# Two heads in one pair of tiles, and values loaded 2 MB at a time, in a decode step with its gradients

## The chip, the cores and the metric

One core of one Trainium2 chip. The metric is the device time of one execution in microseconds (us); lower is better. The number shown for a kernel is the median of its runs.

## What is computed

A decode step (one token, batch of 2) of a block whose attention and bilinear feed-forward part stand side by side, and the gradients of its output with respect to its input, the caches and all weights:

```python
# B, Sq, D = 2, 1, 576; Hq, Hkv, Sk, Dh = 32, 16, 4096, 128; F = 4608; all bfloat16
xn = _layernorm(x, axis=-1)
q = (xn @ wq) per head;  k, v = caches, each shared by 2 query heads
p = softmax(q k^T * Dh**-0.5);  A = (p v) @ wo
B = ((xn @ w_gate) * (xn @ w_up)) @ w_down
out = x + A + B
# outputs: out, and the vjp with grad_out for
#   x, k_cache, v_cache, wq, wo, w_gate, w_up, w_down
```

Each cache is 2 x 16 x 4096 x 128 bfloat16, 32 MB, and is read once. Its gradient has the same size and is written once: each row of it is a sum of outer products, of probabilities (for v) or score gradients (for k) with a vector of the query head.

## The kernel before

**Order.** The function is a set of Python generators (streams). Each yields requests (an operation with an estimated time, a buffer to acquire, an event to wait for), and `Order.run` goes through them while the kernel is built and emits the instructions of each engine in the order in which its model of the engines would start them. So the order on every engine, and on SP's queue, which issues nearly all transfers, is fixed at build time. The model's constants (`LATENCY`, `RATE`, `LAG` and so on), the priorities `PRI`, the places `AT` where weights are loaded and the caps on buffers set that order. `Line.push` models when a transfer lands. `ACQ(tag)` takes one free slot of a ring, `REL` gives it back, `SET` and `WAIT` mark events; the waits on the chip itself follow from the data.

**Buffers.** 16 tiles of 1 MB, [128, 4096] bfloat16 (`big`, `NBIG`), are shared by four users with caps: loads of keys and values (`kv`, 7), their transposed copies (`X`, 15), gradients waiting to be stored (`st`, 4) and the weights of the feed-forward part (`G`, 2).

**Steps.** `NS` = 16 steps: 8 groups of two key heads times 2 batches. In a step, each head's keys and values are loaded (`load_kv`, 1 MB each): partition p holds 32 consecutive positions, a row of 8 KB. `turn` makes a transposed copy with two DVE transposes per tile (line 418). `score` multiplies it with a stationary made by `build_W` (line 1205, into PSUM). `softmax` normalizes; `spread` (lines 1212 and 1213) and a DVE transpose bring the probabilities into `pp`, two blocks of [128, 128]: one as the stationary of the outer products, one of the contraction with the values. `dscore` does the same for the score gradients into `dd`. `contract` (line 1378) multiplies them with the loaded tiles. `outer` and `head_outer` make the gradient of the caches: matmuls (line 1226) with a block diagonal `BD` of 16 blocks, 8 for each head, built by GpSimd (line 1193) with `mask16`; PSUM is copied to `big` tiles by ACT or DVE (`cp`, lines 422 and 424, whichever the model finds earlier) and stored by `put` (line 644) 1 MB at a time. `consts` builds the masks and selectors on DVE before the first step. Beside the steps run the feed-forward part (`mlp`), the projections of a group (`group_front`, `group_back`) and the gradients of the weights (`rows_outer` and others), which share all engines.

Of the kernel before, what the change touches and what calls it, by code (L numbers as in the profile page):

```python
# [9 lines left out]
ALU = mybir.AluOpType  # L10
# [42 lines left out]
class Line:  # L53
    def __init__(self):
        self.end = 0.0

    def push(self, at, work):
        if at > self.end:
            self.end = at + (DRY if at > self.end + 0.3 else 0.0)
        self.end += work  # L60
        return Landing(self.end + LAG + DRIFT * self.end)


class Order:
# [58 lines left out]
    def start(self, s):  # L123
# [15 lines left out]
        if r[0] == "acq":  # L139
            ts = [when(t) for t in self.pool(r[1]).values() if t is not None]  # L140
            if not ts or (r[1] in self.used and self.used[r[1]] >= self.cap[r[1]]):
                return None, None
            return max(s.ready, min(ts)), None
# [9 lines left out]
    def run(self):  # L153
        while self.streams:
# [27 lines left out]
            elif r[0] in ("wait", "gate"):  # L182
                s.ready = t
            elif r[0] == "acq":
                slots = self.pool(r[1])
                if r[1] in self.used:
                    self.used[r[1]] += 1
                i = min((k for k, v in slots.items() if v is not None), key=lambda k: (when(slots[k]), k))
                slots[i] = None
                s.ready = t  # L190
                value = i
            elif r[0] == "dma":
                self.free[e] = t + r[2]
                s.land = self.line.push(t + r[2] + LATENCY, r[3])
# [30 lines left out]
def ACQ(tag):  # L225
    return ("acq", tag)
# [22 lines left out]
def DMA(engine, cost, nbytes, row=8192):  # L249
    return ("dma", engine, cost, 0.01 + RATE * nbytes / 16e3 * (0.03676 + 8.0 / row))  # L250
# [3 lines left out]
NBIG, NGU, NWW, NBD = 16, 1, 6, 3  # L254
CAP = {"kv": 7, "X": 15, "st": 4, "G": 2}
PRI = {
    "turn0": [12127.5, 6592.3, 21769.7, -2605.1, 16027.7, 11327.0, 15999.3, 39550.4, 10382.6, -7734.4, 35538.2,
        24878.1, 2718.9, 31584.2, -26890.5, 2784.8],
    "turn1": [-17638.3, 2610.3, 11642.0, -23025.1, -666.2, 15183.7, -8429.9, 1153.7, -20487.3, 25941.4,
        10117.7, 4947.3, -2272.2, 26485.5, 30929.5, -2450.0],  # L260
    "W0": [17499.7, 23187.9, 23229.4, -24562.1, -25413.4, 21241.8, -52583.1, 25355.3, -4026.7, -26992.9,
        -2792.0, -39509.0, -20712.1, -23397.7, -38581.5, -1973.1],
    "W1": [-68220.0, -3785.6, -5692.6, -26672.7, -32830.2, -16110.0, -12761.0, -19860.2, 22087.6, 15126.8,
        -21980.3, 8805.5, -32643.6, 50340.4, -9766.7, -46949.6],
    "BD0": [33847.1, 15885.5, -3782.4, -11229.3, 24201.3, 31507.4, 16705.2, 36715.7, 22613.4, -26234.1,
        -2581.7, 109848.8, -44765.9, -8040.0, -3442.2, 23039.7],
    "BD1": [6023.1, 63457.9, 25871.9, 3200.3, 32198.5, -18814.1, 12365.4, 26532.9, 45847.1, -51895.6, 27362.3,
        -76393.3, 2863.2, -15443.1, -42340.1, -14044.7],
    "att": [-30329.0, -12134.6, -9680.1, 2262.2, -4349.2, 5413.2, -20317.8, -14023.7, -15815.4, -22206.1,
        -49797.4, -334.9, -19593.2, -20211.8, -68161.8, -27358.0],  # L270
    "dsc": [-23906.4, -34630.7, -2728.5, -23998.0, -19328.5, -8575.3, -10061.5, -15550.8, 13655.4, -23902.2,
        -28324.1, -40880.7, -28538.6, -56867.0, -5830.5, -12006.5],
    "conv": [-12341.8, -11809.0, -28772.8, 4652.6, -75297.7, -7012.1, -20664.5, 17461.5, 27449.8, 21658.4,
        -6850.8, -13921.3, -10206.6, -13431.8, 19855.6, -8570.5],
    "con": [-42900.2, 17788.3, 198.2, -17106.1, -21976.4, -3999.9, 7207.3, -22623.4, -6927.6, 21516.2, 20924.0,
        -13390.2, -118243.2, -7700.5, 19019.7, 14780.5],
    "out0": [22678.2, 12788.2, 42398.2, 31027.3, 49279.4, -11087.6, 5917.5, 42793.0, -20399.7, 57105.8,
        29375.6, 687.4, 24906.2, -2550.4, -27276.1, 33869.5],
    "out1": [19262.8, 2604.4, 2928.7, 23228.2, 21627.8, -10501.4, 15188.8, 7961.4, 18967.4, 20607.5, 11898.0,
        33332.1, 33685.2, 22220.0, 30731.2, 4846.1],  # L280
    "load": [27975.6, -31596.9, -27237.7, 3512.0, -22563.4, -17007.1, 4137.9, 25122.5, 5758.3, -9052.6,
        -35105.2, 2003.7, -28928.7, 6812.9, 23298.4, -60102.7],
    "front": [22268.9, 9016.8, -3195.4, -925.0, -11488.9, -5594.5, -10266.7, 2816.4],
    "back": [8334.8, 3131.5, 10704.4, -20159.0, -16008.9, -4698.0, -5371.8, 1371.3],
    "mlp": [-5535.1, -15193.4, -221.7, -14784.7, -3773.2, 8812.5, 807.2, 180.8, 6936.3],
    "mload": [-52363.2, -31069.0, 25120.7, -76464.9, 11215.5],
    "wload": [26545.8, -25483.3, -28807.4, 17849.2, -51701.7, -14210.9, -857.7, -9350.9, -12979.9, -24368.0,
        -173571.7, -10429.5, -11015.2, 13337.1, -10805.0, 6634.5],
    "wout": [-3917.3],
    "store": [6257.1],  # L290
    "fin": [-45349.8],
    "const": [46567.9],
}
AT = {
    "wq": [-5, 7, 11, 24, 31, -18, 50, -5],
    "wo": [-13, -2, -15, 2, 36, -14, 47, 53],
    "mlp": [2, 16, -13, 39, 111],
}
LATENCY, DRY, RATE = 0.5, 0.9, 1.009
LM, LAG, DRIFT = 0.67, 2.2, 0.009  # L300
CLK = 1.65
BIAS = 0.21111771427708687
SLACK = {"PE": 0.0, "ACT": 0.11786185086953341, "DVE": 0.44815392421950667, "POOL": 1e9, "SP": 1e9}
# [7 lines left out]
def kernel(  # L311
# [35 lines left out]
    WW = 40  # L347
# [20 lines left out]
    kv_t = X_t = st_t = G_t = tiles("big", NBIG, [P, NCH * Dh])  # L368
# [5 lines left out]
    BD_t = tiles("BD", NBD, [P, 16, Dh])  # L374
    vr_t = tiles("vr", 2, [P, Dh])
    W_t = [tiles(f"W{t}", 2, [P, 4, G, WW]) for t in range(2)]
# [14 lines left out]
    pp_t = tiles("pp", 2, [P, 2, P])  # L391
    dd_t = tiles("dd", 2, [P, 2, P])
# [3 lines left out]
    for i in range(2):  # L396
# [4 lines left out]
            ds=const.tile([P, P], BF16, name=f"ds{i}"), sp=const.tile([P, 2 * P], BF16, name=f"sp{i}")))  # L401
        ch_t[i]["mr"] = ch_t[i]["sp"][0:1].bitcast(FP32)
# [66 lines left out]
    identP = const.tile([P, P], BF16, name="identP")  # L469
# [4 lines left out]
    S64 = ch_t[0]["ex"][:, 0:64]  # L474
    G4 = const.tile([P, 32, 4], FP32, name="G4")
    mask8 = const.tile([P, 4, 2], FP32, name="mask8")
    mk16 = ch_t[0]["ex"][:, 64:80].rearrange("p (l c) -> p l c", l=2)
    mask16 = const.tile([P, 16], BF16, name="mask16")
# [8 lines left out]
    def consts():  # L487
# [3 lines left out]
        def sums(t, dims, off=0, src=identf):  # L491
            nc.vector.reduce_sum(t, view(src[:], 0, P, off, dims), axis=AX.X)

        yield DVE(0.6)
        sums(K4[:], [[1, 4], [4, 32]])
        nc.vector.tensor_copy(G4[:], view(K4[:], 0, P, 0, [[0, 32], [1, 4]]))
        yield DVE(0.7)
# [1036 lines left out]
```

## Time and profile before

| | |
|---|---|
| median of 3 runs | 471.11 us (470.17 to 472.08) |
| profiled execution: time / span | 471.37 / 469.6 us |
| mean granted TensorE clock | 0.71 |
| bytes read and written | 92.48 MB each |

The span runs from the first to the last instruction of the profiled execution. A profile names an engine's work by line: L1226 is line 1226 of the kernel. PE is TensorE's matmul, PEld its weight load, DVE VectorE, ACT ScalarE, POOL GpSimd and SP SyncE, whose queue (SPq) issues the transfers. In a group, the number after the bar is busy time in all, then the mean of one in ns, then the idle time just before it and what ended that.

### The profile page before, as it was taken

To read this page: it belongs to the slowest core of one execution; us is meant where nothing else is said; L and a number is where in the kernel's file an instruction comes from. 1 tells how busy PE (TensorE), PEld (TensorE's weight loads), DVE (VectorE), ACT (ScalarE), POOL (GpSimd) and SP (SyncE) were. 2 spreads that over 40 slices of the span, in tenths; PEclk is the share of its full clock that TensorE was granted. 3 is DMA by queue.
4 is the path that set the end of the run, shared out by engine and by line. 5 is a ranking of instruction groups with operands and counts; after the bars stand their busy time and mean duration, and the time that the engine had idled before them with its cause. 6 is when DMAs were issued, how large, how long until landed. Compare 5 with 4: busy or idle time off the path is not lost.

```text
span 469.6 us, 15459 instructions
## 1 busy us (share of the span) xinstructions
PE 370.8 (79%) x6636; PEld 217.5 (46%) x6636; DVE 369.5 (79%) x705; ACT 334.3 (71%) x507; POOL 146.8 (31%) x176
## 2 busy tenths in 40 slices
PE   0588688869887777986997669789699898998984
PEld 0455444435653352554463444564345434444453
DVE  9689878967867879688689658978867978898772
ACT  2149668867885948671798638877678678789973
POOL 3350242681330320203252264000843705325100
PEclk9978897767757668776675767956656658566977
DMA  8999999999999999999999999999999989999995
GB/s 317 404 413 403 363 390 419 409 416 421 418 416 420 399 421 406 412 415 419 399 418 404 386 418 424 408 413 342 413 416 393 424 270 416 423 413 413 424 368 176
DMA packets 40053, 185.96 MB, mean 396 GB/s; under 512 B 3496, under 2 KB 11184, under 8 KB 23600
## 3 DMA queue, kind: packets, MB, share of 16 engines
q1 hardware_dynamic: 39976, 184.96, 98.1%
q8 instruction: 52, 0.85, 0.7%
q14 instruction: 17, 0.14, 0.1%
q10 hardware_dynamic: 8, 0.00, 0.0%
HBM read 92.48 MB, written 92.48 MB: 394 GB/s over the span
## 4 chain that ended last, share of the span: by engine, by line
PE 42%; ACT 18%; DVE 18%; DMA 12%; issue 5%; POOL 2%; SPq 2%; ACTq 0%; DVEq 0%; POOLq 0%
ACT big L422 15%; DMA out_dram<-big 10%; DVE big L418 8%; PE ps_m L1378 8%; PE ps_o L1226 7%; PE ps_m L1205 7%; PE ps_o L675 4%; PE ps_m L841 3%; DVE big L424 3%; DMA big<-in_A_v_cache_dram 3%; PE ps_m L967 2%; PE ps_m L636 2%; POOL BD L1193 2%; PE ps_o L712 1%; SPq L1129 1%
## 5 line engine op out<-in xcount | busy, mean ns | idle before, releaser
L422 ACT CAST big<-ps_o 128x1024 bf16<-128x1024 f32 (+4 forms) x319 | 279.7, 950 | 40.3 <-PE ps_o L1226 18.2
L418 DVE STREAM_TRANSPOSE big<-big 128x1024 f32<-128x1024 f32 x146 | 176.1, 1223 | 5.9 <-DMA big<-in_A_v_cache_dram 3.6
L1193 POOL TENSOR_TENSOR BD<-vr,mask 128x2048 bf16<-128x2048 bf16 x32 | 115.2, 3603 | 198.8 <-ACT vr L422 122.2
L424 DVE CAST big<-ps_o 128x1024 bf16<-128x1024 f32 (+2 forms) x71 | 78.2, 1102 | 15.8 <-PE ps_o L675 5.2
L1205 PE MATMUL ps_m<-big,W 128*32 128x128 bf16 x2048 | 57.1, 274 | 5.5 <-ACT osb L422 0.7
L1226 PE MATMUL ps_o<-BD,dd 32*128 32x512 bf16 x256 | 48.8, 489 | 12.7 <-ACT big L422 9.2
L1205 PEld LDWEIGHTS <-W 128*32 128x32 bf16 x2048 | 45.4, 121 | 21.9 <-issue 18.6
L1226 PE MATMUL ps_o<-BD,pp 32*128 32x512 bf16 x256 | 42.1, 461 | 10.4 <-ACT big L422 6.7
L1170 POOL COPY W<-rep 32x16 bf16<-32x16 bf16 x128 | 24.5, 192 | 63.5 <-DVE rep L951 53.2
L418 DVE STREAM_TRANSPOSE big<-ww 128x1152 f32<-128x1152 f32 (+1 forms) x25 | 32.9, 1317 | 4.5 <-DMA out_dram<-big 3.3
L1378 PE MATMUL ps_m<-big,pp 128*32 128x512 bf16 x256 | 28.2, 536 | 1.5 <-DVE small L1330 1.2
L1378 PE MATMUL ps_m<-big,dd 128*32 128x512 bf16 x256 | 27.5, 518 | 1.5 <-DVE dd L418 0.6
L1226 PEld LDWEIGHTS <-dd 32*128 32x128 bf16 x256 | 11.8, 97 | 32.4 <-issue 24.7
L1226 PEld LDWEIGHTS <-pp 32*128 32x128 bf16 x256 | 10.4, 95 | 26.9 <-issue 22.6
L422 ACT CAST osb<-ps_m 128x512 bf16<-128x512 f32 x15 | 8.9, 590 | 15.9 <-PE ps_m L1378 12.6
L675 PE MATMUL ps_o<-dyr,R 32*32 32x288 bf16 x256 | 17.3, 402 | 2.0 <-ACT big L422 2.0
L675 PE MATMUL ps_o<-dyr,hb 32*32 32x288 bf16 x288 | 16.5, 346 | 1.1 <-ACT big L422 0.9
L967 PE MATMUL ps_m<-big,Wdy 128*128 128x128 bf16 x144 | 14.9, 285 | 3.1 <-DVE small L1283 2.0
L712 PEld LDWEIGHTS <-xnr 32*128 32x128 bf16 x368 | 12.5, 119 | 9.3 <-issue 8.6
L422 ACT CAST sp<-ps_m 128x256 bf16<-128x256 f32 x22 | 8.4, 380 | 11.2 <-PE ps_m L1213 11.0
L636 PEld LDWEIGHTS <-wm 128*32 128x32 bf16 x704 | 13.4, 115 | 6.3 <-issue 5.1
L841 PE MATMUL ps_m<-big,Wdy 128*128 128x128 bf16 x162 | 15.6, 272 | 0.6 <-DVE small L1291 0.4
(210 smaller groups left out, 481.9 us busy)
## 6 DMA issues: line engine op xcount, KB each, us to landing
out_dram<-big SPq DMA_DIRECT2D x74, 1024.0 KB, 12.1
big<-in_A_k_cache_dram SPq DMA_DIRECT2D x32, 1024.0 KB, 12.4
big<-in_A_v_cache_dram SPq DMA_DIRECT2D x32, 1024.0 KB, 12.5
out_dram<-big SPq DMA_DIRECT2D x17, 576.0 KB, 11.4
ww<-in_B_w_down_dram SPq DMA_DIRECT2D x9, 576.0 KB, 11.1
ww<-in_A_wo_dram SPq DMA_DIRECT2D x8, 576.0 KB, 11.1
ww<-in_A_wq_dram SPq DMA_DIRECT2D x8, 512.0 KB, 11.6
big<-in_B_w_gate_dram SPq DMA_DIRECT2D x4, 1024.0 KB, 13.1
```

The lines of the kernel that those rows point to most:

```text
L418: nc.vector.transpose(out, in_)
L422: nc.scalar.copy(out, in_)
L424: nc.vector.tensor_copy(out=out, in_=in_)
L636: nc.tensor.matmul(dp[32 * q:32 * q + 32, :], lhsT=view(Wm[:], 0, P, 8 * pos(q, s), [[1, 32]]), rhs=view(X, 0, P, xoff(q, s), [[FS, blocks ...
L675: nc.tensor.matmul(o[32 * q:32 * q + 32, aa, 0:HD2], lhsT=view(t, 32 * q, 32, 2 * A + aa, [[4, 32]]), rhs=dyr[32 * q:32 * q + 32, k * HD2: ...
L841: nc.tensor.matmul(dh, lhsT=Wdy[:, e, 2 * k:2 * k + P], rhs=view(X[:], 0, P, 64 * k + e, [[D, FC], [2, 32]]), start=(k == 0 and e == 0), s ...
L967: nc.tensor.matmul(dp, lhsT=Wdy[:, e, 2 * k:2 * k + P], rhs=view(X[:], 0, P, 64 * k + e, [[D, GH], [2, 32]]), start=(k == 0 and e == 0), s ...
L1170: nc.gpsimd.tensor_copy(view(W_t[t][w][:], 32 * a, 32, 6 + 8 * a, [[G * WW, 4], [WW, G], [1, 2]]), view(rep_t[grp[g]["qs"]][:], 32 * a, 32 ...
L1193: nc.gpsimd.tensor_tensor(BD_t[i][:], view(vr_t[v][:], 0, P, 0, [[0, 16], [1, Dh]]), view(mask16[:], 0, P, 0, [[1, 16], [0, Dh]]), ALU.mult)
L1205: nc.tensor.matmul(sc[32 * cq:32 * cq + 32, :], lhsT=view(W[:], 0, P, (be * G + l) * WW + 6 - 4 * c2 - 2 * l, [[1, 32]]), rhs=view(X[:], 0 ...
L1226: nc.tensor.matmul(o[:, k, :], lhsT=pr2[32 * c4:32 * c4 + 32, :], rhs=BD[32 * c4:32 * c4 + 32, 8 * l + 4 * h2:8 * l + 4 * h2 + 4, :], star ...
L1378: nc.tensor.matmul(ct[32 * j:32 * j + 32, :], lhsT=view(rT, 0, P, 4 * c + 2 * l, [[1, 32]]), rhs=kv_t[kvS[s][t][l]][:, Dh * c:Dh * (c + 4) ...
```

## The change

A step's two heads now share a pair of neighbouring `big` tiles: each head has 64 partitions and 64 consecutive positions in each, a row of 16 KB, of which the first tile of the pair holds the first half and the second the second. With `JOINED`, the values of every step are one transfer of 2 MB in rows of 16 KB, for which two neighbouring slots are taken at once. Keys are two transfers of 1 MB and the gradients' stores two of 1 MB, in rows of 8 KB that lie 16 KB apart (`PAIRED`, for stores of 2 MB, is empty). Since a tile now has both heads, 64 partitions each, the block diagonal has 8 blocks in place of 16 for the same matmuls; the stationary of the scores has no index for the head; and the spread makes three matmuls, of 128, 128 and 256 columns, into four blocks of `pp` and `dd`, so that its copy and its transpose have 512 columns. There are 4 `BD` tiles (3 before), caps of 8 for `kv` and 6 for `st`, other constants and masks, and two clocks in `Line`, one with dearer stores. All priorities, the places of the weights and the model's constants are other numbers, so the order is another one on every engine.

```diff
 class Line:
...
-    def push(self, at, work):
-        if at > self.end:
-            self.end = at + (DRY if at > self.end + 0.3 else 0.0)
-        self.end += work
-        return Landing(self.end + LAG + DRIFT * self.end)
+    def push(self, at, work, more):
+        for k, w in enumerate((work, work + more)):
+            if at > self.end[k]:
+                self.end[k] = at + (DRY if at > self.end[k] + 0.3 else 0.0)
+            self.end[k] += w
+        return Landing(max(self.end[0] + LAGM, self.end[1] + LAG))
...
+                if r[2] == 2:
+                    i = min((k for k in range(0, len(slots) - 1, 2) if slots[k] is not None and slots[k + 1] is not None),
+                            key=lambda k: (max(when(slots[k]), when(slots[k + 1])), k))
+                    slots[i] = slots[i + 1] = None
+                    value = [i, i + 1]
...
-NBIG, NGU, NWW, NBD = 16, 1, 6, 3
-CAP = {"kv": 7, "X": 15, "st": 4, "G": 2}
+NBIG, NGU, NWW, NBD = 16, 1, 6, 4
+JOINED = [range(0), range(16)]
+PAIRED = [range(0), range(0)]
+CAP = {"kv": 8, "X": 15, "st": 6, "G": 2}
 PRI = {
...
-LM, LAG, DRIFT = 0.67, 2.2, 0.009
+LM, LAG, LAGM, SLOW = 0.67, 2.0, 3.2, 0.065
...
-    kv_t = X_t = st_t = G_t = tiles("big", NBIG, [P, NCH * Dh])
+    H2 = NCH * Dh
+    pair_t = [const.tile([P, H2 * min(2, NBIG - 2 * i)], BF16, name=f"big{i}") for i in range((NBIG + 1) // 2)]
+    kv_t = X_t = st_t = G_t = [pair_t[i // 2][:, H2 * (i % 2):H2 * (i % 2) + H2] for i in range(NBIG)]
...
-    BD_t = tiles("BD", NBD, [P, 16, Dh])
+    BD_t = tiles("BD", NBD, [P, 8, Dh])
...
-    pp_t = tiles("pp", 2, [P, 2, P])
-    dd_t = tiles("dd", 2, [P, 2, P])
+    pp_t = tiles("pp", 2, [P, 4, P])
+    dd_t = tiles("dd", 2, [P, 4, P])
...
-        nc.vector.tensor_copy(identP[:].rearrange("p (a c i) -> p a c i", a=4, i=8),
-                              view(ident[:], 0, P, 0, [[8, 4], [32, 4], [1, 8]]))
...
+        for j in range(2):
+            for a in range(4):
+                nc.vector.tensor_copy(view(identP[:], 0, P, P * j + 32 * a + 2 * (a // 2), [[8, 4], [4, 2], [1, 2]]),
+                                      view(ident[:], 0, P, 16 * (a // 2) + 4 * (a % 2) + j, [[32, 4], [2, 2], [8, 2]]))
...
-    views = [A.rearrange("b h (p c) d -> b h p (c d)", p=P) for A in (A_k_cache, A_v_cache)]
-    oviews = [A.rearrange("b h (p c) d -> b h p (c d)", p=P) for A in (out_2, out_3)]
+    def both(A):
+        def rows(b, g, j=None):
+            ap = A[b, G * g:G * g + G].rearrange("h (p c) d -> (h p) (c d)", p=P // G)
+            return ap if j is None else ap[:, j * H2:(j + 1) * H2]
+        return rows
+
+    views, oviews = [both(A) for A in (A_k_cache, A_v_cache)], [both(A) for A in (out_2, out_3)]
...
             for t in range(2):
-                for l in range(G):
-                    yield PRIO(pr("load", s) if n else -1e5)
-                    i = yield ACQ("kv")
-                    yield DMA("SP", 0.36, 1 << 20)
-                    nc.sync.dma_start(kv_t[i][:], views[t][b, G * g + l])
-                    kvS[s][t][l] = i
-                    yield ("lset", kvL[s][t][l])
+                yield PRIO(pr("load", s) if n else -1e5)
+                if s in JOINED[t]:
+                    kvS[s][t] = i = yield ACQ("kv", 2)
+                    yield DMA("SP", 0.36, 2 << 20, 16384)
+                    nc.sync.dma_start(pair_t[i[0] // 2][:], views[t](b, g))
+                for j in range(2):
+                    if s not in JOINED[t]:
+                        kvS[s][t][j] = i = yield ACQ("kv")
+                        yield DMA("SP", 0.36, 1 << 20)
+                        nc.sync.dma_start(kv_t[i], views[t](b, g, j))
+                    yield ("lset", kvL[s][t][j])
...
-                    view(W_t[t][w][:], 32 * a, 32, 6 + 8 * a, [[G * WW, 4], [WW, G], [1, 2]]),
-                    view(rep_t[grp[g]["qs"]][:], 32 * a, 32, t * 8 * GH + b, [[2 * GH, 4], [4, G], [2, 2]]))
+                    view(W_t[t][w][:], 32 * a, 32, 3 + 16 * (a // 2) + 4 * (a % 2), [[WW, 4], [8, 2]]),
+                    view(rep_t[grp[g]["qs"]][:], 32 * a, 32, t * 8 * GH + b + 4 * (a // 2), [[2 * GH, 4], [2, 2]]))
...
-                nc.gpsimd.tensor_tensor(BD_t[i][:], view(vr_t[v][:], 0, P, 0, [[0, 16], [1, Dh]]),
-                                        view(mask16[:], 0, P, 0, [[1, 16], [0, Dh]]), ALU.mult)
+                nc.gpsimd.tensor_tensor(BD_t[i][:], view(vr_t[v][:], 0, P, 0, [[0, 8], [1, Dh]]),
+                                        view(chunk8[:], 0, P, 0, [[1, 8], [0, Dh]]), ALU.mult)
...
-                        lhsT=view(W[:], 0, P, (be * G + l) * WW + 6 - 4 * c2 - 2 * l, [[1, 32]]),
+                        lhsT=view(W[:], 0, P, be * WW + 3 - 2 * c2 - l, [[1, 32]]),
...
     def spread(src, dst_ps):
-        nc.tensor.matmul(dst_ps[:, 0:P], lhsT=identP[:], rhs=src[:], start=True, stop=True)
-        nc.tensor.matmul(dst_ps[:, P:2 * P], lhsT=src[:], rhs=identP[:], start=True, stop=True)
+        for j in range(2):
+            nc.tensor.matmul(dst_ps[:, j * P:j * P + P], lhsT=identP[:, j], rhs=src[:], start=True, stop=True)
+        nc.tensor.matmul(dst_ps[:, 2 * P:4 * P], lhsT=src[:], rhs=identP[:].rearrange("p j n -> p (j n)"), start=True, stop=True)
...
-                    nc.tensor.matmul(o[:, k, :], lhsT=pr2[32 * c4:32 * c4 + 32, :],
-                                     rhs=BD[32 * c4:32 * c4 + 32, 8 * l + 4 * h2:8 * l + 4 * h2 + 4, :],
+                    nc.tensor.matmul(o[:, k, :], lhsT=pr2[32 * c4:32 * c4 + 32, 2 + j, :],
+                                     rhs=BD[32 * c4:32 * c4 + 32, 4 * h2:4 * h2 + 4, :],
...
-        e = yield EV(256)
-        cp(e, c["sp"][:], m_t[m][:, 0:2 * P])
+        e = yield EV(512)
+        cp(e, c["sp"][:], m_t[m][:])
...
-        yield WAIT(Ezero, grp[g]["EoT"])
+        yield WAIT(Ezero, grp[g]["EoT"], *kvL[s][t])
...
-                    nc.tensor.matmul(ct[32 * j:32 * j + 32, :], lhsT=view(rT, 0, P, 4 * c + 2 * l, [[1, 32]]),
+                    nc.tensor.matmul(ct[32 * j:32 * j + 32, :], lhsT=view(rT[:], 0, P, P * l + 4 * c, [[1, 32]]),
```

More of the change, by code (lines that the diff above doesn't have):

```diff
@@ L139, in start @@
         if r[0] == "acq":
-            ts = [when(t) for t in self.pool(r[1]).values() if t is not None]
-            if not ts or (r[1] in self.used and self.used[r[1]] >= self.cap[r[1]]):
+            slots = self.pool(r[1])
+            if r[2] == 2:
+                ts = [max(when(slots[k]), when(slots[k + 1])) for k in range(0, len(slots) - 1, 2)
+                      if slots[k] is not None and slots[k + 1] is not None]
+            else:
+                ts = [when(t) for t in slots.values() if t is not None]
+            if not ts or (r[1] in self.used and self.used[r[1]] + r[2] > self.cap[r[1]]):
                 return None, None
@@ L306, in pr @@
+SLACK = {"PE": 0.0, "ACT": 0.23032757015772898, "DVE": 0.42253244122742706, "POOL": 1e9, "SP": 1e9}
 def pr(name, i=0):
@@ L468 @@
     identf = const.tile([P, P], FP32, name="identf")
-    identP = const.tile([P, P], BF16, name="identP")
+    identP = filled("identP", [P, 2, P], BF16, 0.0)
     selA = const.tile([P, 4, 4, 32], BF16, name="selA")
@@ L642, in put @@
         for d, x in zip(dst, src):
-            yield DMA("SP", 0.36, nbytes, row)
+            yield DMA("SP", 0.36, nbytes, row, store=True)
             nc.sync.dma_start(d, x)
-        yield ("lrel", tag, slot)
+        for i in slot if isinstance(slot, list) else [slot]:
+            yield ("lrel", tag, i)
     def unit(mms, pe, cols, ev, done, quad=None, kind="r"):
```

202 lines of the change are left out of this document (107 added, 95 removed).

## The prediction

> **What bounds the kernel now.** I read the page first, from the busy shares to the DMA queues and the chain.
>
> ```profile
> span 469.6 us, 15459 instructions
> PE 370.8 (79%) x6636; PEld 217.5 (46%) x6636; DVE 369.5 (79%) x705; ACT 334.3 (71%) x507; POOL 146.8 (31%) x176
> DMA  8999999999999999999999999999999989999995
> q1 hardware_dynamic: 39976, 184.96, 98.1%
> q8 instruction: 52, 0.85, 0.7%
> HBM read 92.48 MB, written 92.48 MB: 394 GB/s over the span
> PE 42%; ACT 18%; DVE 18%; DMA 12%; issue 5%; POOL 2%; SPq 2%; ACTq 0%; DVEq 0%; POOLq 0%
> ```
>
> No engine is busy for more than 79% of the span, while the packets of the one data queue fill 98.1% of the sixteen DMA engines' time. So the transfers set the time, and the engines matter where they let the queue run dry. The digit row shows only a dip near the end and the last slice. To see how much is lost, and where, I asked for stretches in which the page's GB/s row is low, beside two good ones.
>
> ```profile
> core 0: us, PE busy (x) PEld busy (x) DVE busy (x) ACT busy (x) POOL busy (x), PEclk, DMA share, GB/s
> 48.00:54.00 6.00, 3.68 (x92) 2.26 (x84) 5.16 (x11) 4.50 (x9) 0.00 (x0) 1.00 0.96 320
> 182.00:190.00 8.00, 6.19 (x50) 3.26 (x50) 5.84 (x11) 5.33 (x9) 2.35 (x1) 0.61 1.00 381
> 318.00:328.00 10.00, 9.13 (x176) 4.30 (x176) 8.50 (x16) 7.09 (x10) 0.00 (x0) 0.67 0.95 331
> 374.00:386.00 12.00, 11.22 (x137) 4.82 (x138) 8.47 (x18) 8.79 (x14) 1.02 (x1) 0.54 0.82 279
> 420.00:430.00 10.00, 8.43 (x116) 3.70 (x114) 8.81 (x16) 9.81 (x14) 5.52 (x2) 0.67 1.04 400
> 440.00:450.00 10.00, 8.80 (x169) 4.71 (x168) 9.12 (x17) 10.00 (x15) 0.00 (x0) 1.00 1.01 424
> 450.00:469.60 19.60, 11.87 (x258) 8.52 (x258) 9.22 (x24) 9.31 (x14) 0.00 (x0) 0.67 0.64 241
> ```
>
> The last two columns are the DMA share and the rate. A full queue moves 424 GB/s. Measured against that, 48 to 54 loses 6 x (1 - 320/424) = 1.5 us, 182 to 190 0.8, 318 to 328 2.2 and 374 to 386 4.1: 8.6 us in four holes. The end, from 450 on, loses 19.6 x (1 - 241/424) = 8.5 us. In the two deeper holes PE is busy 91% and 94% at a granted clock of 0.67 and 0.54: there PE, and not the queue, is the bound for a few microseconds. Who stood in front of the queue in the deepest hole is told by the waits of SP's own queue, asked from 368 to 392 (in all, times, longest):
>
> ```profile
> SPq L1087 <- PE ps_m L1378: 7.8, 1, 7.8
> SPq L1087 <- DVE big L418: 5.4, 1, 5.4
> SPq L644 <- DVE big L424: 5.0, 1, 5.0
> ```
>
> SP issues in program order. L1087 is the load of keys and values, which stood 7.8 us for a slot that a contraction (L1378) had to give back, and everything behind it stood too.
>
> **The change part by part. Packets.** Two stretches of ten microseconds with the same DMA engines, one all rows of 8 KB, one with many small rows, give the price of a packet:
>
> ```profile
> DMA packets 1859, 4.00 MB, mean 400 GB/s; under 512 B 106, under 2 KB 1184, under 8 KB 1709
> ...
> DMA packets 581, 4.24 MB, mean 424 GB/s; under 512 B 64, under 2 KB 64, under 8 KB 64
> out_dram<-big SPq DMA_DIRECT2D x74, 1024.0 KB, 12.1
> big<-in_A_k_cache_dram SPq DMA_DIRECT2D x32, 1024.0 KB, 12.4
> big<-in_A_v_cache_dram SPq DMA_DIRECT2D x32, 1024.0 KB, 12.5
> ```
>
> The first is 420 to 430, the second 440 to 450. The first moves 0.24 MB less, which is 0.24/4.24 of 10 x 1.01 x 16 = 162 us of engine time, or 9.1 us, and has 1278 packets more: 7 ns for each. The values are 32 transfers of 128 rows of 8 KB, 4096 packets; in rows of 16 KB there are 2048. 2048 x 7 ns over 16 engines is **0.9 us less**. It is nothing if a row of 16 KB still goes as two packets. At most the whole shortfall of the span, 469.6 x (1 - 394/424) = 33 us, is a matter of packets: 33 x 16/39976 = 13 ns each, 1.7 us in all.
>
> **Transfers.** Sixteen transfers fewer. By their packets of completion alone, 16 x 16 x 7 ns over 16 engines, they are worth **0.1 us**. If instead all of the 33 us were a cost per transfer, spread over the 138 of 1 MB quoted, each would cost 0.24 us and sixteen would save 3.9. I take 0.1, since 440 to 450 runs such transfers at a share of 1.01 with no time between them. The Trainium skill ("DMA: Bandwidth & Descriptors", section Bandwidth) measures 341 GB/s for a transfer of 1 MB, 6.15 us, and 425 for one of 16 MB, and makes batches of at least 1 MiB a rule; going by its figures, an estimate for 2 MB is 11.0 us against 12.3 for two of 1 MB, and sixteen of them would save some 21 us. The trace doesn't bear that out here, where several are in flight.
>
> **Engine work.** These groups carry the prices (busy and mean ns stand after the bar):
>
> ```profile
> L1193 POOL TENSOR_TENSOR BD<-vr,mask 128x2048 bf16<-128x2048 bf16 x32 | 115.2, 3603 | 198.8 <-ACT vr L422 122.2 <-PE ps_o L1226 33.7 <-PE ps_o L712 17.2
> L1170 POOL COPY W<-rep 32x16 bf16<-32x16 bf16 x128 | 24.5, 192 | 63.5 <-DVE rep L951 53.2 <-PE ps_m L1205 5.7
> L418 DVE STREAM_TRANSPOSE pp<-sp 128x256 bf16<-128x256 bf16 x16 | 7.0, 440 | 2.3 <-ACT sp L422 2.2
> L418 DVE STREAM_TRANSPOSE Xt<-gu 128x512 f32<-128x512 f32 x9 | 6.1, 678 | 0.0
> L422 ACT CAST sp<-ps_m 128x256 bf16<-128x256 f32 x22 | 8.4, 380 | 11.2 <-PE ps_m L1213 11.0
> L422 ACT CAST osb<-ps_m 128x512 bf16<-128x512 f32 x15 | 8.9, 590 | 15.9 <-PE ps_m L1378 12.6
> L424 DVE CAST sp<-ps_m 128x256 bf16<-128x256 f32 x10 | 4.1, 408 | 0.5 <-PE ps_m L1213 0.4
> L424 DVE CAST big<-ps_o 128x1024 bf16<-128x1024 f32 x57 | 68.9, 1208 | 8.3 <-PE ps_o L1226 4.4 <-PE ps_o L712 2.6 <-issue 0.7
> L1212 PE MATMUL ps_m<-pr,identP 128*128 128x128 bf16 x16 | 4.5, 280 | 2.2 <-DVE rep L951 1.1 <-ACT vr L422 0.4 <-DVE accx L912 0.3
> L1378 PE MATMUL ps_m<-big,pp 128*32 128x512 bf16 x256 | 28.2, 536 | 1.5 <-DVE small L1330 1.2
> ```
>
> POOL's block diagonal has half the columns: 32 x 1.8 = 58 us of busy time go, and the 128 copies for W shrink a little. Hardly any of it reaches the end. POOL is idle 69% of the span, its builds mostly stood waiting for their input, and in the hole from 318 it does nothing. I take 0. The chain gives POOL 2%, 9.4 us, so half of that, 4.7, is the most that can be won; a loss is excluded, as the same buffers are ready sooner.
>
> The spread of the probabilities, twice in each of 16 steps, gets wider. Its DVE transpose has 512 columns in place of 256; the nearest row of that width is 678 ns, so 32 x 0.24 = 7.7 us (14.1 if it simply doubles). The copy out of PSUM goes from 380 to the 590 ns of the 512-column row on ACT, 22 x 0.21 = 4.6 us, and on DVE from 408 to some 675 (on the line to 1208 for 1024 columns), 10 x 0.27 = 2.7. PE gets a third matmul of 256 columns, between 280 and 536 ns, some 365: 11.7 us. That is 26.7 us of added work, of which DVE has 10.4, ACT 4.6 and PE 11.7. Beside a full queue it costs nothing. In the four holes, 36 us or 7.7% of the span, I charge it in full: 7.7% of 26.7 is **2.0 us more**. The upper bound takes each engine's share of the chain, 0.18 x 15.0 + 0.42 x 11.7 = 7.6 us; the lower is 0, if the new order puts the spreads beside full stretches.
>
> ```profile
> DVE big L418 <- DMA big<-in_A_v_cache_dram: 3.6, 1, 3.6
> 6.06 0.28 DVE L492 TENSOR_REDUCE ex<-identf 128x64 f32<-128x128 f32 x1
> 6.37 0.32 DVE L492 TENSOR_REDUCE ex<-ex 128x8 f32<-128x32 f32 x2
> 7.79 0.49 DVE L515 COPY selA<-ident 128x128 bf16<-128x128 bf16 x4
> ```
>
> A value's transpose now waits for 2 MB and not for 1: 2.1 MB less 1.05 at 424 GB/s, 2.5 us later for the first half. Behind the waiting transpose stands all of DVE, and behind it PE's scores. It is covered: in the whole span DVE waited for a value load once, 3.6 us. If that cover went, sixteen times 2.5 would be 40 us of DVE waiting. The constants at the start lose the reductions of 0.28 and 0.32 us and gain seven small copies of about 0.12 (the selector's four took 0.49): **0.3 us more**, ahead of the first transposes. The scores, contractions, outer products and stores keep their counts, and the contraction's added wait for both loads names data that its first matmuls read anyway: 0.
>
> **Slots and order.** The pool of big buffers stays at 16, but loads may hold 8 of them (7 before) and stores 6 (4 before). One more load queued ahead of a hole is 1.05 MB / 424 GB/s = 2.5 us of work for the queue. Against the four holes that fills 1.5, 0.8, 2.2 and 2.5: **7.0 us less**. At best all 8.6 go and half of the end's 8.5. At worst none does, or new holes open. This term is the one the trace says least about, since the instructions will stand in another order throughout.
>
> The sum, against the profiled execution's 471.37 us (span 469.6 and 1.8 around it; 0.3 above the median 471.11): 471.37 - 0.9 - 0.1 + 2.0 + 0.3 - 7.0 = **465.7 us**.
>
> **The rivals.** *The pair takes the slot back.* A value load takes two neighbouring slots at once, so the eighth slot is only a place to wait for the pair. For it: L1087's waits are for slots. Then the holes stay: 471.37 - 1.0 + 2.3 = 472.7, no change that can be told.
>
> *SP stands for the second slot.* The pair is issued only when both its slots are free; SP stands one more transfer, 2.5 us, and stores behind it that are ready stand with it. It decides where SP's standing outlasts what is in flight, some 12.5 us from issue to landing; the row of 7.8 us, with the queue already drained, is such a place. Half of the loads are values; two of four holes deepened by 2.5 each: 472.7 + 5.0 = 477.7, slower.
>
> *The wider spread lies on the path.* The hole from 374, PE at 94%, speaks for it; the 98.1% speaks against it elsewhere. With the upper bound and no hole filled: 471.37 - 1.0 + 0.3 + 7.6 = 478.3, slower.
>
> *Every transfer has dead time of its own*, 0.24 us by the row above: 465.7 - 3.8 = 461.9. The skill's rule just cited would have it larger still.
>
> *Rows of 16 KB go slowly.* The one row with packets of 16 KB is q8: 0.7% of 16 x 469.6 over 52 packets is 1.01 us each, against 0.62 for two of 8 KB (8192 B at 424/16 GB/s, twice). 2048 x 0.39/16 = 50 us more, 516. Against it: these are 52 packets on engines that q1 fills to 98.1%, so what they take may be mostly waiting, and between 1 KB and 8 KB q1's own rows show a price per packet and no price per size.
>
> **How the numbers follow.** A measurement of this kernel can tell about 0.5%, 2.4 us, from no change. Forecast 0.59; slot taken back 0.16; second slot 0.13; spread on the path 0.06; dead time 0.04; slow rows 0.02. Faster: 0.59 + 0.04 = 0.63. Same: 0.16. Slower: 0.21. The low end takes all middle holes (1.6 beyond the 7.0), half of the end (4.3) and most of POOL's bound (3): 457. The high end reaches the second-slot case and stops near 478; slow rows and the tails of both sides stay out.
>
> **What would show it.** Right: packets of q1 near 37,700, the four stretches of 320 to 380 GB/s gone or shallower, sp's transpose near 0.68 us, POOL near 90 us busy, mean rate near 399 GB/s. Wrong: long SP waits at the value load, PE at 94% in new dry stretches, a full queue under 415 GB/s in all-large stretches (the rows), or landings of values far over 15 us.

## The result: 4.6% slower, and the profile after

The changed kernel takes 493.35 us (median of 4 runs, 491.08 to 496.24) against 471.60 us before on the same chip (470.17 to 472.69): a ratio of 1.0461, 95% interval 1.0418 to 1.0503. That is 21.75 us slower, where 6 us faster was forecast. The profiled execution took 491.68 us.

These are the lines of its page that answer to those shown of the kernel before: span, busy shares, the tenths of DMA and the rate in 40 slices, the queues, the chain.

```profile
span 489.9 us, 15513 instructions
...
PE 378.5 (77%) x6668; PEld 216.2 (44%) x6668; DVE 380.8 (78%) x714; ACT 338.5 (69%) x504; POOL 95.3 (19%) x176
...
DMA  8999999999999999799999989999959969989995
GB/s 324 402 414 420 357 352 378 415 420 419 423 404 411 413 429 420 315 338 396 426 430 358 391 342 398 418 417 416 385 246 329 391 235 385 423 314 377 422 410 220
...
q1 hardware_dynamic: 37672, 184.96, 94.9%
...
HBM read 92.48 MB, written 92.48 MB: 378 GB/s over the span
...
PE 41%; DVE 24%; ACT 17%; DMA 12%; issue 6%; POOL 0%; DVEq 0%; ACTq 0%
```

The bytes are the same and there are 2304 packets fewer, yet the queue fills 94.9% of its time and not 98.1%. Two deep dips stand in the last third of the GB/s row (246 and 235). The deepest dip of the kernel before, the hole from 374 of the prediction, is shallower (270):

```profile
GB/s 317 404 413 403 363 390 419 409 416 421 418 416 420 399 421 406 412 415 419 399 418 404 386 418 424 408 413 342 413 416 393 424 270 416 423 413 413 424 368 176
```

Set against a full queue of 424 GB/s, the whole span loses 489.9 x (1 - 378/424) = 53.2 us; before it lost 469.6 x (1 - 394/424) = 33.2. With equal bytes this difference is that of the spans whatever the cause. The queue's shares tell more: in the mean of the sixteen DMA engines, packets took 0.949 x 489.9 = 464.9 us and 25.0 us had none, where before it was 460.7 and 8.9. By this count 16.1 of the 20.3 us are time in which the queue was dry, and 4.2 are packets that took longer in all.

The stretches in which that happens, by the same view as in the prediction (busy time and count of PE, PEld, DVE, ACT and POOL, then clock, DMA share and GB/s), with one full stretch for comparison:

```profile
200.00:212.00 12.00, 10.85 (x241) 6.70 (x233) 11.12 (x18) 9.60 (x15) 1.39 (x1) 0.69 0.74 268
278.00:288.00 10.00, 8.34 (x120) 3.99 (x121) 8.44 (x16) 8.41 (x13) 3.32 (x10) 0.77 0.79 300
318.00:328.00 10.00, 9.54 (x179) 5.72 (x176) 8.96 (x15) 8.87 (x11) 0.00 (x0) 0.66 1.03 416
346.00:370.00 24.00, 5.28 (x90) 2.61 (x91) 7.83 (x8) 3.92 (x5) 0.00 (x0) 0.53 0.76 300
...
388.00:402.00 14.00, 11.97 (x210) 5.95 (x209) 10.63 (x20) 9.49 (x15) 1.89 (x1) 0.62 0.60 226
432.00:446.00 14.00, 12.29 (x219) 5.59 (x215) 12.53 (x20) 12.50 (x16) 1.89 (x1) 0.74 0.84 296
470.00:489.90 19.90, 14.09 (x228) 8.93 (x227) 10.30 (x24) 9.54 (x14) 0.00 (x0) 0.59 0.75 290
```

By the prediction's formula the five holes lose 4.4, 2.9, 7.0, 6.5 and 4.2 us, 25.0 in all, against 8.6 in the four holes before; the end loses 6.3 against 8.5. One stretch is of another kind than the rest: from 346 to 370 every engine is nearly idle (PE busy 5.28 of 24 us, ACT 3.92) and the queue runs dry as well. In each of the other holes some engine is busy. Where none is, one wait may hold everything, and the timelines of that window tell which. First DVE (start, duration, instruction; in brackets the idle time ahead of it and what ended it), then PE, then SP, each from its own answer:

```profile
348.33 1.22 DVE L444 CAST big<-ps_o 128x1024 bf16<-128x1024 f32 x1 [0.70 <-PE ps_o L1252]
364.62 2.37 DVE L438 STREAM_TRANSPOSE big<-big 128x1024 f32<-128x1024 f32 x2 [15.07 <-DMA out_dram<-big]
366.92 0.14 DVE L1440 CAST oT<-ps_m 128x4 bf16<-128x4 f32 x1
```

```profile
367.05 1.05 PE L1234 MATMUL ps_m<-big,W 128*32 128x128 bf16 x32 [15.94 <-DVE oT L1440]
```

```profile
344.91 3.53 SPq L1112 DMA_DIRECT2D big<-in_A_v_cache_dram  x1
348.53 19.64 SPq L663 DMA_DIRECT2D out_dram<-big  x3
368.22 0.45 SPq L1141 DMA_DIRECT2D ww<-in_A_wo_dram  x1
```

DVE wants to transpose into a `big` slot and stands 15.07 us for a **store** out of `big` to land. Behind that transpose stands the small cast of `oT`, and behind the cast PE's scores. SP stands as well, between the first and the second of three gradient stores (L663). It is not held by PE: it goes on at 367.02, just before the scores start, and the waits of SP's own queue name DVE (in all, times, longest):

```profile
367.02 0.52 SPq L663 DMA_DIRECT2D out_dram<-big  x1
...
SPq L663 <- DVE oT L1440: 16.8, 1, 16.8
```

So nothing is added to the queue while DVE waits for the queue's last entries. The DMA view from 344 to 372, in slices of 0.7 us, shows it drain to nothing:

```profile
DMA  9998999799999999999999997522000000499999
GB/s 468 433 421 351 458 309 244 268 398 416 408 413 375 420 405 424 484 467 433 439 439 398 468 427 316 211 111 82 23 0 0 0 0 0 181 404 421 217 336 375
```

A transpose waits for a store where the store still reads the slot that it writes. Before, such waits came to 4.3 us in the whole span; now they are 16.5, nearly all of it this one:

```profile
DVE big L418 <- DMA out_dram<-big: 4.3, 3, 3.3
...
DVE big L438 <- DMA out_dram<-big: 16.5, 2, 15.1
```

But here the store reads another slot. In the code, `tails` stores the last rows of a pair of weight gradients to two destinations, and takes every second partition of its tile for each: `bass.AP(..., [[2 * pstep, 64], [1, n * FS]])`, a pattern that steps over partitions. Before, the tile under that pattern was one slot. Now it is a pair, and the slot that DVE wants is the other half of the same pair. The two touch no byte in common; the wait between them, which is set when the kernel is built, does not see that. In the kernel as built it goes both ways: the two strided stores read the second half of the pair `big2`, the two transposes write its first half and wait for the first of these stores to land, and the second store waits for the transposes. So SP stood for DVE while DVE stood for SP's last store. (The view names the cast of `oT`, which ended next to SP's release; as built, the wait is for the transpose just ahead of it.)

### The profile page after: what moved, and what is told of

Read it like the earlier page. It is cut to its first block, busy times and chain, and to the rows that moved or that the text cites. A ratio compares the mean times of both kernels' runs of the same rounds, so it can differ in the third digit from the quotient of the medians.

```text
span 489.9 us, 15513 instructions
## 1 busy us (share of the span) xinstructions
PE 378.5 (77%) x6668; PEld 216.2 (44%) x6668; DVE 380.8 (78%) x714; ACT 338.5 (69%) x504; POOL 95.3 (19%) x176
## 3 DMA queue, kind: packets, MB, share of 16 engines
q1 hardware_dynamic: 37672, 184.96, 94.9%
## 4 chain that ended last, share of the span: by engine, by line
PE 41%; DVE 24%; ACT 17%; DMA 12%; issue 6%; POOL 0%; DVEq 0%; ACTq 0%
ACT big L442 14%; DVE big L438 13%; PE ps_o L1252 7%; PE ps_m L1234 7%; PE ps_m L1420 6%; DMA out_dram<-big 6%; PE ps_o L695 4%; DVE big L444 3%; PE ps_m L987 3%; DMA big<-in_B_w_up_dram 2%; DMA ww<-in_A_wq_dram 2%; DMA big<-in_A_k_cache_dram 2%; PE ps_m L861 1%; PE ps_m L655 1%; PE ps_o L732 1%
## 5 line engine op out<-in xcount | busy, mean ns | idle before, releaser
L442 ACT CAST big<-ps_o 128x1024 bf16<-128x1024 f32 (+3 forms) x319 | 278.9, 950 | 44.1 <-PE ps_o L1252 30.4
L438 DVE STREAM_TRANSPOSE big<-big 128x1024 f32<-128x1024 f32 x146 | 175.6, 1221 | 19.4 <-DMA out_dram<-big 16.5
L1222 POOL TENSOR_TENSOR BD<-vr,chunk 128x1024 bf16<-128x1024 bf16 x32 | 60.5, 1893 | 132.9 <-ACT vr L442 74.2
L1234 PE MATMUL ps_m<-big,W 128*32 128x128 bf16 x2048 | 60.7, 287 | 22.2 <-DVE oT L1440 16.3
L1234 PEld LDWEIGHTS <-W 128*32 128x32 bf16 x2048 | 48.6, 128 | 37.1 <-issue 34.2
L1252 PE MATMUL ps_o<-BD,pp 32*128 32x512 bf16 x256 | 47.6, 514 | 9.6 <-ACT big L442 7.6
L1199 POOL COPY W<-rep 32x8 bf16<-32x8 bf16 x128 | 27.0, 211 | 139.5 <-DVE rep L971 129.0
L442 ACT CAST sp<-ps_m 128x512 bf16<-128x512 f32 x27 | 16.0, 593 | 16.5 <-PE ps_m L1243 12.6
L442 ACT CAST dof<-ps_m 128x128 bf16<-128x128 f32 x8 | 3.5, 442 | 33.1 <-PE ps_m L987 33.1
L987 PE MATMUL ps_m<-big,Wdy 128*128 128x128 bf16 x144 | 14.7, 282 | 2.6 <-DVE big L438 1.9
L655 PE MATMUL ps_m<-big,wm 128*32 128x128 bf16 (+1 forms) x416 | 12.4, 265 | 5.3 <-DVE D L869 2.6
## 6 DMA issues: line engine op xcount, KB each, us to landing
big<-in_A_v_cache_dram SPq DMA_DIRECT2D x16, 2048.0 KB, 11.2
```

The lines of the kernel that those rows point to most:

```text
L438: nc.vector.transpose(out, in_)
L442: nc.scalar.copy(out, in_)
L655: nc.tensor.matmul(dp[32 * q:32 * q + 32, :], lhsT=view(Wm[:], 0, P, 8 * pos(q, s), [[1, 32]]), rhs=view(X, 0, P, xoff(q, s), [[FS, blocks ...
L987: nc.tensor.matmul(dp, lhsT=Wdy[:, e, 2 * k:2 * k + P], rhs=view(X[:], 0, P, 64 * k + e, [[D, GH], [2, 32]]), start=(k == 0 and e == 0), s ...
L1199: nc.gpsimd.tensor_copy(view(W_t[t][w][:], 32 * a, 32, 3 + 16 * (a // 2) + 4 * (a % 2), [[WW, 4], [8, 2]]), view(rep_t[grp[g]["qs"]][:], 3 ...
L1222: nc.gpsimd.tensor_tensor(BD_t[i][:], view(vr_t[v][:], 0, P, 0, [[0, 8], [1, Dh]]), view(chunk8[:], 0, P, 0, [[1, 8], [0, Dh]]), ALU.mult)
```

## The experiments

Each run is told with the kernel before on the same chip; its median moved between 471.5 and 472.6 us. "Above the kernel before" means above the one run beside it, so that such numbers can be compared.

**The tails on neighbouring partitions.** A second stationary, `xnh`, lets the matmul put the two halves on partitions 0 to 63 and 64 to 127, so that each store is a plain slice. The order stays as it is.

```diff
-            src = [bass.AP(st[:].tensor, st[:].offset + w * pstep, [[2 * pstep, 64], [1, n * FS]]) for w in range(2)]
+            src = [st[64 * w:64 * w + 64, 0:n * FS] for w in range(2)]
```

> The changed kernel in its own order, but the stores of the tails (two stores of 64 rows, out of one big tile) take partitions 0 to 63 and 64 to 127 instead of every second partition. Theory A (false wait): in the changed kernel the pair is one tile, and a store that steps over partitions counts as touching both halves of the pair, so DVE's transposes into the other half wait for it: the 15.1 us in which DVE, PE and ACT stand still from 349.5 go, and the time falls by 12 to 15 us, to 478 to 481. Rival B (the slot itself was late, or the order is merely longer): the same wait stays, 493 within 2 us.

477.56 us, ratio 1.0100 [1.0070, 1.0130]: **15.8 us** come back, a little more than theory A's 12 to 15. The same instructions of DVE stand in the same order, and start 15.1 us earlier; the first of the pair's two stores is issued only when they already run (first DVE, then SP, each from its own answer):

```profile
348.36 1.23 DVE L444 CAST big<-ps_o 128x1024 bf16<-128x1024 f32 x1 [0.70 <-PE ps_o L1254]
349.50 2.36 DVE L438 STREAM_TRANSPOSE big<-big 128x1024 f32<-128x1024 f32 x2
351.78 0.14 DVE L1442 CAST oT<-ps_m 128x4 bf16<-128x4 f32 x1
...
350.85 3.67 SPq L665 DMA_DIRECT2D out_dram<-big  x3
```

So the transposes needed nothing of these stores: neither a late slot nor a longer order was what DVE waited for.

Its page and its windows:

```profile
GB/s 318 402 416 417 369 315 339 423 405 426 416 424 421 392 408 427 421 365 374 422 423 410 369 335 396 398 414 413 394 386 418 419 412 401 419 359 384 423 355 226
...
q1 hardware_dynamic: 37672, 184.96, 97.6%
...
HBM read 92.48 MB, written 92.48 MB: 389 GB/s over the span
```

```profile
278.00:288.00 10.00, 9.34 (x113) 4.11 (x113) 8.48 (x16) 7.87 (x10) 3.97 (x10) 0.50 0.79 306
346.00:370.00 24.00, 16.86 (x234) 9.45 (x230) 18.18 (x27) 9.28 (x19) 6.24 (x12) 0.57 1.02 399
...
373.00:387.00 14.00, 12.34 (x210) 6.10 (x201) 10.23 (x20) 9.13 (x14) 1.89 (x1) 0.50 1.01 421
...
388.00:402.00 14.00, 11.81 (x173) 5.80 (x166) 10.96 (x22) 12.14 (x18) 1.70 (x8) 0.70 1.01 402
...
417.00:431.00 14.00, 12.19 (x226) 5.61 (x225) 12.73 (x20) 12.99 (x17) 1.89 (x1) 0.76 0.94 338
```

Both dips are gone, the one of the stall (300 to 399 GB/s) and the one 40 us after it (226 to 402; the work of that stretch now stands some 15 us earlier, from 373, at 421). So the second went with the first. The hole from 278 stays, and so does the one from 432, now from 417. The one from 200, ahead of the stall, is shallower too (361 in place of 268); no run tells why. So 15.8 of the 21.75 us are one wait between halves that have nothing to do with each other. This kernel is still 5.3 above the kernel before; the two don't add up to 21.75 because the kernel before itself took 0.65 more when it was run beside this one.

**Values as two transfers of 1 MB.** On top of the last kernel, each value load becomes two loads of rows of 8 KB, issued at the same place.

```diff
-                    nc.sync.dma_start(pair_t[i[0] // 2][:], views[t](b, g))
+                    for j in range(2):
+                        nc.sync.dma_start(kv_t[i[j]], views[t](b, g, j))
```

> As e1, but each value load is issued as two transfers of 1 MB in rows of 8 KB, one for each tile of the pair, at the same place in SP's queue. Theory C (the 2 MB transfers cost): rows of 16 KB took 661 ns on average against 2 x 321 for two of 8 KB, 2.4 us over the 2048, and the first half of a pair can be turned 2.5 us sooner; the time falls by 2 to 10 us against e1. Theory A with B: the transfers are not what costs; within 2 us of e1, or slower by 1 us for the packets and issues that come back.

479.16 us, ratio 1.0154 [1.0110, 1.0197], beside 1.0100 [1.0070, 1.0130]: with two transfers it is 1.6 us longer, and the intervals still touch.

```profile
q1 hardware_dynamic: 39976, 184.96, 97.7%
...
big<-in_A_v_cache_dram SPq DMA_DIRECT2D x32, 1024.0 KB, 12.2
```

The packets are those of before again, and the time is not. So the large transfers in rows of 16 KB are not what costs. What they are worth is not told from nothing: 1.6 us by the medians and 2.5 by the ratios, whose intervals leave room for 0 to 5 us. The Trainium skill ("DMA: Bandwidth & Descriptors", section Bandwidth) gives larger transfers a higher rate, from which the prediction worked out an estimate of 21 us; this run bears out its sign at most, not its size, where several transfers are in flight.

**The spread's transposes twice.** Each of the 32 transposes into `pp` and `dd` is issued a second time, 32 x 0.70 = 22.4 us of DVE work.

```diff
         t32(pp_t[S["pp"]][:].rearrange("p t n -> p (t n)"), c["sp"][:])
+        t32(pp_t[S["pp"]][:].rearrange("p t n -> p (t n)"), c["sp"][:])
```

> As e1, but each transpose of the spread (32 of them, 0.69 us each) is done twice: 22 us of DVE work more at the place where the change added 8. Theory D (the added engine work lies on the path): most of it shows, 15 to 22 us more than e1, so that the change's own 8 us of transposes would account for 5 to 8. Rival (covered by the queue): under 8 us more, so the change's own share is under 3.

492.61 us, ratio 1.0419 [1.0362, 1.0477]: 15 us more than without. Two thirds of the added work shows, in a kernel whose queue is 97.6% full.

**The spread at its old width**, without the order being touched: 256 columns copied and transposed, two matmuls.

```diff
-        nc.tensor.matmul(dst_ps[:, 2 * P:4 * P], lhsT=src[:], rhs=identP[:].rearrange("p j n -> p (j n)"), start=True, stop=True)
...
-        cp(e, c["sp"][:], m_t[m][:])
+        cp(e, c["sp"][:, 0:2 * P], m_t[m][:, 0:2 * P])
```

> As e1, in the same order, with the spread cut back to the width it had before the change: two matmuls of 128 columns, a copy and a transpose of 256 columns; the outer products and the contraction take their stationaries from the two blocks that are left, so the gradients of the caches and what hangs on the contraction are left out of the computation. It takes away 8 us of DVE transposes, some 6 us of copies on ACT and DVE and 11 us of PE. Theory D (added engine work on the path): e1 stood 1.0% above the kernel before, and two thirds of 22 us of doubled transposes showed; 8 us of DVE at two thirds is 5.5, and some of the copies and matmuls beside it: the time falls by 5 to 10 us, to the kernel before or under it (468 to 473). Rival E (the order alone is longer): within 2 us of e1, 476 to 479.

476.87 us, ratio 1.0092 [1.0054, 1.0129], against 1.0100 with the wide spread. Nothing comes back, although the transposes fall from 0.69 to 0.42 us:

```profile
L438 DVE STREAM_TRANSPOSE pp<-sp 128x256 bf16<-128x256 bf16 x16 | 6.8, 424 | 0.8 <-ACT sp L442 0.8
```

So most of the 5.3 us is not the added engine work: the two intervals would hide a gain of at most some 2.7 us. Doubling the transposes costs 15 us, and removing what the change added gains nothing that can be told: there is no one price per microsecond here.

**The kernel before with its transposes twice**, 32 x 0.44 = 14.1 us of DVE work, by the same added line.

> The kernel before, with each of its 32 transposes of the spread (0.44 us each) done twice: 14 us more on DVE. The prediction held that the transfers set the time and charged added engine work at 7.7%: that would be 1 us. If the kernel before was as near to its engines as the changed one (68% of the doubled work showed in e3), it is 8 to 11 us.

474.34 us, ratio 1.0041 [1.0019, 1.0064]: 1.7 us of 14. In this order the prediction's way of charging (in the holes only, 7.7%, which makes 1.1) is about right.

**A new order for the changed kernel, with and without the strided tails.** What is left is the order. All priorities, places of weights and some of the model's constants are found anew for the kernel with plain tails; its plan (the end that the builder's own model foresees) becomes 464.7 us, where the changed kernel's was 470.7. The second run is the same order with the tails as the change has them.

```diff
 PRI = {
-    "turn0": [37975.1, 382.4, 46237.8, -36324.1, 17554.1, 26048.8, 43068.0, 77427.9, -5308.2, -5965.2, 81053.0,
+    "turn0": [21689.14, 63106.86, 51036.65, -5349.1, 57275.36, 52343.68, 79370.75, 81612.68, 141468.37, 60359.16, 138406.83, -106618.39, 296813.69, -33402.89, -14090.8, -211600.75],
...
```

> e1 with another order: priorities, places of the weights and two constants of the order's model found anew, with the model's surcharge on stores at 0.04 in place of 0.065. The model's own end is 464.7 us, against 470.7 for the order of the changed kernel. Theory E (what is left of the loss is the order): the chip follows the model's end, e1's 477.6 less 3 to 7, 471 to 475. Rival (the layout itself costs): no change against e1, 476 to 479.

> The changed kernel as it is, tails included, in the order of e6. Theory A: the false wait is there wherever the order puts something into the other half of a pair from which such a store has not landed, so its price hangs on the order: anything between nothing and 15 us above e6. If it costs the same 15 here, it is a matter of the stores and not of the place.

474.67 us, ratio 1.0053 [1.0035, 1.0071]: 2.7 us above the kernel before are left, so 2.6 of the 5.3 were order. The stretch from 278 runs at 415 GB/s in it. With the strided tails it is 479.14 us, ratio 1.0144 [1.0117, 1.0171]. The wait between the halves is there again, elsewhere and shorter:

```profile
168.52 1.25 DVE L424 STREAM_TRANSPOSE big<-big 128x1024 f32<-128x1024 f32 x1 [7.10 <-DMA out_dram<-big]
```

So the same wait costs 4.5 us in this order and 15.8 in the other: its price is that of the place where it falls.

**The kernel before in other orders.** Once with its priorities jostled at random (a plan of 470.5 us in place of 462.3), once with an order found by the search that served the changed kernel (a plan of 460.8). The code of the steps is untouched in both.

> The kernel before with every priority moved by a random amount (standard deviation 300, where they are some 10,000 to 70,000 apart); buffers, tiles and operations are the same, and the order's model ends at 470.5 us in place of 462.3. Theory E: the order alone moves the time by as much as the model says, 6 to 10 us more than the kernel before. Rival (small moves of the order are absorbed by the full queue): within 2 us of it.

> The kernel before with priorities found anew for it; the model's end is 460.8 us in place of 462.3. Theory E: the time falls by 0 to 3 us. Rival: any new order loses on the chip what the model cannot see, 2 us or more above the kernel before.

Jostled: 481.09 us, ratio 1.0187 [1.0172, 1.0202], 9.1 us for an order alone, with the same work, bytes and packets (twelve copies went from ACT to DVE with it). Its row of rates has the sign of it, dips to 298 and 271 in slices where the kernel before moved 421 and 419:

```profile
GB/s 308 406 414 399 379 379 423 393 421 298 303 420 423 396 419 424 424 338 271 422 416 423 417 410 416 322 417 414 413 404 424 421 318 409 424 413 416 426 379 171
```

Searched: 473.97 us, ratio 1.0037 [1.0021, 1.0052], 2.0 us slower, although its plan ends 1.5 us earlier. A plan's end tells an order with 8 us of difference, and not one with 2. Beside the changed kernel in its new order (1.0053 [1.0035, 1.0071]) the intervals overlap: with orders of the same search, the two layouts can't be told apart.

**The new order, with the spread doubled and narrowed.** The two edits of before, made on the kernel in its new order.

> The kernel with the order found anew and the tails on 64 neighbouring partitions (474.7 us, 2.5 above the kernel before), with each transpose of the spread made twice: 32 more of about 0.69 us, 22 us of work on VectorE, nothing else changed. In the older order the same addition cost 15 us. Theory P (an edit's price hangs on the slack that the order leaves at its place): another price here, outside 12 to 18 us, so below 486.7 or above 492.7 us. Rival Q (the price belongs to the edit: two thirds of the work shows in any order of this layout): 12 to 18 us, 486.7 to 492.7 us, with 489.7 as the middle.

> The same kernel with the spread cut back to the width before: two matmuls of 128 columns, 256 columns copied and transposed (what hangs on the second half of the blocks is left out, so the gradients of the caches and what follows from the contraction are not the reference's). Theory D' (the 2.5 us that are left above the kernel before are the engine work that the wider spread added, 7.7 on VectorE, about 6 in copies and 11 on TensorE): they come back, 472.2 us or less. Rival E' (what is left lies in the order's length and its slack): nothing comes back, 473.7 to 475.2 us.

Doubled: 482.91 us, ratio 1.0236 [1.0211, 1.0262]; 22.4 us of DVE work cost 8.2 (8.7 with each set against the kernel before that was run beside it), where they cost 15 in the other order. Narrowed: 475.48 us, ratio 1.0071 [1.0047, 1.0096]; again nothing comes back, and the time is 0.3 above the end of what was expected for that case. The price of an edit hangs on the order around it, and the last 2.7 us are not the spread.

## Why the prediction was wrong

These groups and issues of the changed kernel answer to the terms (busy and mean ns after the bar; for the transfer, KB and us to landing):

```profile
L438 DVE STREAM_TRANSPOSE pp<-sp 128x512 bf16<-128x512 bf16 x16 | 11.1, 693 | 2.2 <-ACT sp L442 2.2
L442 ACT CAST sp<-ps_m 128x512 bf16<-128x512 f32 x27 | 16.0, 593 | 16.5 <-PE ps_m L1243 12.6 <-PE ps_m L968 2.0 <-DVE small L1309 1.3
L444 DVE CAST sp<-ps_m 128x512 bf16<-128x512 f32 x5 | 3.4, 676 | 0.6 <-PE ps_m L1243 0.6
L1243 PE MATMUL ps_m<-identP,pr 128*128 128x256 bf16 x16 | 5.8, 362 | 0.0
L1222 POOL TENSOR_TENSOR BD<-vr,chunk 128x1024 bf16<-128x1024 bf16 x32 | 60.5, 1893 | 132.9 <-ACT vr L442 74.2 <-DVE vr L444 31.7 <-PE ps_o L1252 13.3
big<-in_A_v_cache_dram SPq DMA_DIRECT2D x16, 2048.0 KB, 11.2
```

- **The missing term: 15.8 us.** The step that failed worst is the one that costed the stores at nothing because they "keep their counts". The diff makes two slots one tile, and the prediction looked at what that does to loads and slots, but not at who else shares the tile. Two stores with a pattern over every second partition tie the two halves together, and that costs 15.8 us where the prediction put 0. No rival named it; two of them looked for a wait of SP at a load, and it came on DVE, and on SP at a store.
- **Slots and order, -7.0: wrong in sign.** With the false wait gone the change is still 5.3 us above the kernel before. The four stretches that the prediction named did fill: without the false wait they run at 353, 416, 420 and 425 GB/s, which by its formula is a gain of 7.3 us. But new holes opened that cost more, of which the one from 278 stands without the false wait too (306 GB/s). So the step that failed is to count the filled holes as a gain of the whole. Whether the larger caps filled them or the other order did is not shown; no run puts the caps back. The prediction said that this term is the one the trace tells least about, gave "new holes open" as its worst case, and then took 7.0 of the 8.6 us that the holes could give. The jostled order shows the scale that belongs there: 9.1 us from the order alone. In a new order 2.6 of the 5.3 go, and 2.7 stay.
- **Engine work, +2.0 within 0 to 7.6: not contradicted.** The sizes were right: 0.693 us for the transpose (0.678 taken), 0.593 and 0.676 for the copies (0.590 and 0.675), 0.362 for the third matmul (0.365). Narrowing the spread changed the time by -0.7 in one order and by +0.8 in the other, both within the noise: the lower end of the range. The doubled transposes show that this is no law, nor is "beside a full queue it costs nothing": 12% of the added work was seen in the order before, 67% and 37% in the two others. The rival with the spread on the path, at 7.6 us, is out.
- **Packets and transfers, -1.0: not contradicted.** 37,672 packets (37,700 forecast); splitting the values again gave +1.6 us with intervals that touch. The price of 7 ns for a packet takes both stretches at a DMA share of 1.01, where the first had 1.04; with that it is 11 ns, and the term 1.4 in place of 0.9, which changes nothing. The rival of slow rows (50 us) is out by far: a stretch of loads and stores ran at 416 GB/s, and 2 MB landed in 11.2 us. Dead time per transfer did not bring the time that it forecast, but as a price it is not excluded: sixteen transfers more would cost 3.8 us, and splitting the values cost between 0 and 5.
- **POOL, 0: fits.** It fell from 146.8 to 95.3 us busy, 51.5 against the 58 taken: half the columns took 1.89 us and not half of 3.60, and the copies for W became longer (27.0 us in place of 24.5). This was not undone by itself, nor were the constants.
- **The two rivals of the slots.** In the one big stall SP stood at a store and not at a value load, so neither is what made the result. Nor do they show in what is left: without the false wait SP's waits at loads of keys and values come to 80.2 us in all, and before to 79.6. That the time then lies at the second slot's 477.7 is chance as far as this tells. No run tests them alone, since the split loads still take both slots at once.

Together, the wait of 15.8 us that stood at 0, and slots and order, where some 5 us of loss stood as 7.0 of gain, make up the miss. What stays open is the last 2.7 us: whether this layout needs a longer order, or the search stopped short of a better one. The runs say only that the kernel before, given an order of the same search, loses 2.0 too. No version run here beats the kernel before.

## What to carry to other kernels

When two buffers become one tile, list every instruction that reads or writes either half with a pattern that is not a plain slice; one pair of strided stores here tied the halves and cost 15.8 us, and plain slices took that back. In a kernel whose queue is 98% full, look first for the stretch in which all engines are idle at once: here it had one cause, and a later hole went with it. Where an order is fixed at build time, a change that remakes it carries an uncertainty of its own, 9 us of 472 here, larger than any term of this sum; it belongs into the range as a case, not into the sum as a gain.

## What the runs showed of the hardware

A queue that ran dry did not only lose the time in which it was dry. The stall lost 7.0 us of transfer from 346 to 370, and 6.5 more in a hole from 388 to 402, which vanished with it; how the one led to the other is not shown. And engine work beside a full queue is not free by rule: the same 22.4 us of DVE work cost 15 us in an order whose queue share was 97.6% and 8.2 us in one of 97.7%, so that the share did not tell the slack.
